# Half-width products in A's last stage, fourteen C blocks by crossbar loads, chunk 13 in quarters

## The chip, the cores and the metric

The kernel runs on one core of a Trainium2 chip. The metric is the device time of one execution in microseconds. Engines named here: PE (matrix products; "PEld" its weight loads), DVE (vector engine), ACT (scalar engine, which here mostly copies results from the matrix engine's banks to on-chip memory: an eviction), POOL and SP, of which both issue transfers. SP's queue issues loads and the last stores, POOL's the stores in between.

## The reference

Two heads over S = 2048 positions and D = 1024 channels stand side by side in the output, A in the left 1024 columns and B in the right ones.

```python
# A: a short causal filter, a product, a long convolution by FFT over 2S, a skip, a gate
for t in range(4):
    k_shift = k_shift + k_pad[:, t:t + S, :] * shift_k[:, 3 - t]
kv = k_shift * v
y = irfft(rfft(pad(kv)) * rfft(pad(ssm_k)))[:, :S, :]
a = q * (y + kv * ssm_D)
# B: a diagonal complex recurrence between two matrix products
Lam_bar = exp(dt * Lam);  B_bar = ((Lam_bar - 1) / Lam)[:, None] * Bmat
Bu = einsum("bld,pd->blp", x, B_bar)
h[t] = Lam_bar * h[t - 1] + Bu[:, t]
b = 2 * einsum("blp,dp->bld", h, Cmat).real + x * Dskip
out = concatenate([a, b], axis=-1)          # (1, 2048, 2048) bf16
```

## The kernel before

**Head B** goes through x in 16 chunks of 128 positions. `x` loads a chunk transposed (a crossbar load, L425). `U.i.jp.jl` multiplies it with B (16 products of 128x128x128, L444), `ue` evicts. On DVE, `r1`/`r2` rotate the result (L459, L466), `cy` on ACT carries the last column of the chunk before (L468), two `sc` are the scans (L472), `r3`/`r4` rotate back (L459, L478). `y.i.dh.part` multiplies with C and adds the diagonal skip (four products of 128x128x512 and one of 128x128, L527 and L530), `ye` evicts, `yst`, `ysp` or `yh` store. For chunks 6 to 12, `yt.i.s.part` does the same in quarters of the matrix engine: sixteen products of 64x64x512 (L498), after the last part of a half sixteen of 64x64x64 (L512). Between the halves s = 0 and s = 1 two row groups change banks; the kernel waits there for an eviction named by `yf`, or, where no `yf` stands, for a drain of PE (L488).

**B and C** come as 128x1024 blocks. Each of the sixteen B blocks is loaded (`bl`, L402), transposed by eight products with the identity (`bT`, L397) and evicted (`bc`, L413). C has sixteen blocks (d = 0..7, real and imaginary): eight go the same way (`cl` L417, `cT` L397, `cc` L421), eight by a crossbar load straight into place (`cx`, L419). All y and yt of an output half need the four d blocks of that half.

**Head A** has three stages with a trip through DRAM after each of the first two. Stage one: `kp`, `vp` load k and v; `kvm`, `kva`, `kvb`, `kvc` on DVE make kv for each of 16 slices n2 (L563 to L578); `am` is the first transform (L583), `ae` evicts, `ast` stores to `Ys_kv` (POOL, L592). The filter goes through `hl`, `hT`, `hc`, `hm`, `he`, `hst` to `Ys_h`. Stage two: `lh`, `lk` reload by frequency (SP, L639; each needs all sixteen stores), `sh`, `sk` transform (L650), `she`, `ske` evict (L660, L667), `sw` swaps rows by a transfer (POOL, L671), `pr` multiplies on DVE (L677), `sa` is the first half of the way back (L689), `sae` evicts, `vst` stores to `Vs` (L700). Stage three: `vl` reloads one n2 (SP, L705; each needs all sixteen stores), `a3` is the last transform with the constant `Gt` (two products of 128x128x512 per half, L717), `a3e` evicts (L724), `qp` loads q (L710), `qm` and `qh` gate on DVE (L726, L730), `osp` and `oh` store (SP, L734, L732).

`Gt[:, p, :]` holds nonzero columns only where the column's parity is p; the two products of an `a3` fill all 128 columns each and add up in one bank.

What sets the order is `ORDER`, a list of some 1,500 words written into the program. Each word is one task; the letters and numbers behind a colon give the slots that it takes: `a` a unit of a 53-unit arena in on-chip memory, `p` one of eight banks, `w` a weight slot, `h` a state slot. Each engine runs its tasks in the order of the list and waits only for data and slots, so the list is every engine's queue.

Of the kernel before, what the change touches and what calls it, by code (L numbers as in the profile page):

```python
# [16 lines left out]
BF16 = mybir.dt.bfloat16  # L17
# [15 lines left out]
def a_constants():  # L33
# [6 lines left out]
    G = np.stack([tr.T * (m % 2 == p)[None, :] * 2 / NFFT for p in range(2)], axis=1)  # L40
# [31 lines left out]
bc.3.0 bl.1.1:a44 bT.1.1:p3 sin1 kva.2 kvb.2:a34 bl.7.1:a46 bT.7.1:p4 bc.3.1 bl.4.0:a45 bT.4.0:p6 bl.7.0:a1 U.0.1.1 bc.1.1 U.0.0.1 bc.7.1 bT.7.0:p7
bc.4.1 bc.4.0 kvb.1:a1 sin2 x.5:a32 U.5.0.0:a50p3 U.5.0.1 U.5.1.0:p4 U.5.1.1 U.5.3.0:p6 bc.7.0 U.5.3.1 U.0.3.1 bl.5.1:a33 bT.5.1:p1 eo ue.5.1 vp.1:a48
bc.5.1 kp.-2 kvm.0:a44 kvc.2 ue.0.3 cl.0.1:a10 kvc.3 cl.1.1:a11 cT.1.1:p7 x.1:a0 U.1.0.0:a48p4 bl.5.0:a9 cx.5.1 kva.0 ue.5.0 bT.5.0:p1 bc.5.0 U.1.0.1
ue.1.0 cT.0.1:p2 cc.0.1 ue.5.3 U.1.2.0:p1 U.1.2.1 cc.1.1 U.1.3.0:p4 U.5.2.0:p6 U.0.2.0:p2 U.0.2.1 stt z2 U.5.2.1 z1 ue.0.1 x.2:a37 ue.0.0 kp.2
kvm.5:a28 kvm.4:a8 vp.0:a38 kvc.1 U.2.0.0:a42p3 U.2.2.0:p7 kvb.0:a36 U.2.3.0:p5 U.2.3.1 U.1.1.0:p0 cl.1.0:a40 kva.4 ue.0.2 r1.0:a4 ue.1.2 ue.5.2 kva.5
gz U.1.1.1 r2.0:h0 dd U.2.1.0:p2 ue.2.3 cx.4.0 am.1.0:p6p5 kvb.5:a41 cx.6.1 rt U.1.3.1 cl.0.0:a33 cT.0.0:p1 sc.0.1 U.2.1.1 ae.1.1.0:a2 ue.1.1 cc.0.0
cl.3.0:a16 cT.3.0:p5 ue.1.3 U.2.2.1 sc.0.0 r1.1:a28 ue.2.1 am.3.1:p4p1 cx.7.0 cc.3.0 ae.1.0.0 r3.0:a16 r2.1:h1 am.1.1:p2p0 ae.1.1.1 r4.0 U.2.0.1
ue.2.0 kvc.0 cT.1.0:p5 cl.2.0:a44 cT.2.0:p6 cc.1.0 x.3:a45 U.3.0.0:a46p0 U.3.2.0:p3 cc.2.0 cl.2.1:a5 cT.2.1:p5 U.3.0.1 cc.2.1 cl.3.1:a4 cT.3.1:p6
ae.3.0.1:a48 ue.2.2 U.3.2.1 ae.1.0.1 am.2.0:p4p5 cc.3.1 U.3.1.0:p2 cx.6.0 U.3.3.0:p7 y.0.0.0:p6 y.0.0.1 r1.2:a16 U.3.3.1 cx.7.1 cy.1 ae.2.0.0:a6  # L80
sc.1.1 sc.1.0 ae.2.1.0 am.2.1:p4p5 ue.3.3 ae.2.0.1 ue.3.0 y.0.0.2 y.0.0.3 kvb.4:a44 am.0.0:p4p7 r3.1:a28 ue.3.2 ae.0.0.0:a4 ae.0.1.0 U.3.1.1 cx.5.0
cx.4.1 y.0.1.0:p0 ue.3.1 vp.2:a38 y.0.1.1 y.0.1.2 kp.3 ae.2.1.1 y.0.1.3 am.3.0:p3p4 kvc.5 am.0.1:p7p2 r4.1 ae.0.0.1 ae.3.1.0 y.1.0.0:p5 ae.0.1.1
ae.3.1.1 kvc.4 y.1.1.0:p7 am.4.0:p4p2 y.1.0.1 y.1.1.1 r2.2:h2 y.1.1.2 hl.1:a42 y.1.1.3 r1.3:a8 ye.0.0:a40 y.1.0.2 cy.2 ae.3.0.0 sc.2.1 am.4.1:p1p3
ae.4.1.0:a38 y.1.0.3 ast.2 sc.2.0 hl.0:a34 r3.2:a28 hl.2:a6 r4.2 r2.3:h0 ye.0.1 ye.1.1:a33 am.5.0:p6p2 ae.4.0.0 ae.4.0.1 ae.4.1.1 ye.1.0 ae.5.0.0:a0
hl.3:a16 hT.0.6:p4 hT.0.5:p7 hc.0.5:a52 ae.5.1.0 hT.0.7:p0 hT.0.3:p5 hT.0.2:p1 hT.0.1:p3 hm.0.5.1:p6p7 x.13:a36 kp.4 y.2.1.0:p2 y.2.1.1 hc.0.2:a44
kvm.8:a28 he.0.5.1.1:a18 he.0.5.1.0 cy.3 hm.0.5.0:p1p7 lw.3:w1 sc.3.0 y.2.0.0:p6 kvm.9:a8 y.2.0.1 sc.3.1 kva.8 y.2.0.2 yst.0 y.2.1.2 he.0.5.0.1
hc.0.1:a52 he.0.5.0.0 kva.9 am.5.1:p7p3 ae.5.0.1 hT.0.4:p1 y.2.1.3 hc.0.4:a47 ast.3 ld_G hT.0.0:p7 ae.5.1.1 y.2.0.3 hc.0.6:a46 ye.2.1:a48 ast.1 xs.13
hm.0.2.0:p3p1 he.0.2.0.0:a2 x.4:a40 U.4.0.0:a6p4 U.4.0.1 ue.4.0 ye.2.0 U.4.1.0:p2 he.0.2.0.1 x.12:a49 hst.0.5.1 hc.0.7:a41 ast.4 U.4.1.1 hm.0.2.1:p3p4
U.4.3.0:p1 U.4.3.1 hst.0.5.0 U.4.2.0:p6 U.4.2.1 yst.1 r3.3:a36 kvb.8:a33 kvb.9:a44 r4.3 kvm.7:a8 ast.0 he.0.2.1.1 ue.4.1 xs.12 hc.0.3:a49
hm.0.3.1:p4p0 he.0.2.1.0 kvm.6:a28 y.3.0.0:p2 ue.4.3 he.0.3.1.0:a34 ue.4.2 he.0.3.1.1 hm.0.1.1:p3p5 he.0.1.1.1:a42 hm.0.3.0:p1p4 y.3.1.0:p6  # L90
hm.0.4.0:p0p5 y.3.1.1 kva.7 x.14:a16 he.0.3.0.1 hc.0.0:a49 kva.6 he.0.1.1.0 hm.0.1.0:p4p7 lw.2:w3 y.3.0.1 he.0.3.0.0 he.0.1.0.1 he.0.1.0.0
# [8 lines left out]
he.1.6.0.0:a46 hst.0.4.1 he.1.6.0.1 hm.1.6.1:p7p4 hT.1.3:p6 he.1.0.0.1:a44 hm.1.0.1:p0p5 he.1.0.0.0 kva.10 hst.0.4.0 hT.1.4:p3 y.4.0.2 he.1.6.1.0  # L100
hT.1.7:p7 hc.1.3:a41 he.1.0.1.0 y.4.1.3 he.1.6.1.1 hc.1.7:a33 hst.0.3.1 he.1.0.1.1 hst.0.0.0 hst.0.0.1 vp.5:a4 kvb.10:a0 kp.7 kvm.11:a8 kva.11 x.6:a35
kvb.11:a34 kvc.11 am.11.1:p0p4 am.11.0:p6p7 y.4.0.3 ae.11.1.1:a30 ae.11.0.1 hT.1.5:p5 ae.11.1.0 ae.11.0.0 kvc.10 am.10.0:p4p0 ae.10.0.0:a4 hst.0.6.0
ae.10.1.0 U.6.0.0:a2p7 am.10.1:p6p4 U.6.0.1 ye.4.0:a34 hm.1.1.0:p0p2 ye.4.1 he.1.1.0.1:a18 ast.6 U.6.2.0:p1 U.6.2.1 he.1.1.0.0 hst.1.6.0 hm.1.3.0:p0p2
# [4 lines left out]
hm.1.4.1:p2p5 he.1.4.1.0 vp.7:a44 vp.6:a30 he.1.3.1.0 y.5.0.1 y.5.0.2 y.5.0.3 ye.5.1:a52 hm.1.5.1:p4p6 he.1.4.1.1 he.1.7.0.0 hm.1.5.0:p7p1
he.1.5.0.1:a40 kvm.12:a36 he.1.5.0.0 kvc.15 kva.12 am.15.1:p3p5 x.7:a46 U.7.0.0:a8p2 he.1.5.1.0 U.7.0.1 ye.5.0 lw.0:w2 am.15.0:p1p7 kvc.13 U.7.1.0:p0
he.1.5.1.1 am.13.0:p4p6 ue.7.0 ast.10 kvb.12:a16 kvm.14:a36 ae.15.0.1:a32 hst.1.1.0 ae.15.1.0 am.13.1:p2p3 x.9:a11 ae.13.1.0:a4 kvc.12 U.9.0.0:a30p7  # L110
U.9.0.1 ae.13.0.1 U.7.2.0:p6 ae.13.1.1 U.7.2.1 x.15:a10 hst.1.2.0 am.12.0:p3p2 ae.13.0.0 ae.15.0.0 kva.14 U.7.1.1 r1.6:a12 kvb.14:a0 r2.6:h0 kvc.14
am.14.0:p4p1 cy.6 ae.12.1.0:a2 ae.12.0.0 sc.6.1 ue.9.0 U.7.3.0:p2 am.14.1:p7p3 hst.1.7.1 ue.7.2 U.9.2.0:p6 ae.15.1.1 ae.14.0.1:a44 U.7.3.1 hst.1.1.1
hst.1.2.1 ue.7.1 hst.1.3.1 am.12.1:p7p0 U.9.1.0:p5 U.9.1.1 ae.14.1.1 ae.14.0.0 ae.14.1.0 U.9.2.1 ue.7.3 ae.12.1.1 hst.1.4.1 hst.1.3.0 sc.6.0 yst.4
# [53 lines left out]
def full_kernel(ctx, tc, A_q, A_k, A_v, A_shift_k, A_ssm_k, A_ssm_D, B_x, B_Lre, B_Lim, B_Bre, B_Bim,  # L167
# [631 lines left out]
```

## Time and profile before

| | |
|---|---|
| three timed runs | 348.27, 350.30, 350.78 us; median 350.3 |
| the profiled execution | 351.36 us, of it 349.6 between the first and the last instruction; granted PE clock 0.995 |
| PE, DVE, ACT, POOL busy | 334.9, 314.1, 285.2, 79.4 us |
| transfers | 103.07 MB; hardware queue 63.98 MB, software queue 38.42 MB |

A row of groups names the line, engine, operation, output and inputs, how many, then busy us and the mean ns of one, and after the bar the idle time before them:

```profile
L472 DVE TENSOR_TENSOR_SCAN gslot<-rtab,gslot 128x1040 bf16<-128x1040 f32 x32 | 73.0, 2310 | 3.0 <-ACT gslot L468 2.8
L717 PE MATMUL bank<-arena,Gt 128*128 128x512 bf16 x62 | 14.5, 379 | 0.1
L421 ACT COPY CT<-bank 128x1024 bf16<-128x1024 bf16 x8 | 8.3, 1052 | 1.0 <-PE bank L397 1.0
```

A product's 379 ns runs from its start to its modelled end; since products overlap, the distance from one start to the next is what the engine pays, and that is read from the chain or the timeline. An instruction of SP or POOL that issues a transfer is shown with the time for which it held that queue; the landing comes later.

### The profile page before, as it was taken

To read this page: it belongs to the slowest core of one execution; us is meant where nothing else is said; L and a number is where in the kernel's file an instruction comes from. 1 tells how busy PE (TensorE), PEld (TensorE's weight loads), DVE (VectorE), ACT (ScalarE), POOL (GpSimd) and SP (SyncE) were. 2 spreads that over 40 slices of the span, in tenths; PEclk is the share of its full clock that TensorE was granted. 3 is DMA by queue.
4 is the path that set the end of the run, shared out by engine and by line. 5 is a ranking of instruction groups with operands and counts; after the bars stand their busy time and mean duration, and the time that the engine had idled before them with its cause. 6 is when DMAs were issued, how large, how long until landed. Compare 5 with 4: busy or idle time off the path is not lost. (4 is left out here: it accounts for less than half of the span.)

```text
span 349.6 us, 10684 instructions
## 1 busy us (share of the span) xinstructions
PE 334.9 (96%) x4540; PEld 236.7 (68%) x4561; DVE 314.1 (90%) x240; ACT 285.2 (82%) x547; POOL 79.4 (23%) x130
## 2 busy tenths in 40 slices
PE   5899999999999999999987999999999999999996
PEld 3799998546765767748863565786668676865442
DVE  4899999999999999999996997979985968997992
ACT  6999997468698999987884889999998887537672
POOL 5000000032334337055231004223233151300100
PEclk9999999999999999999998999999999999999999
DMA  6999967599999999999869599989989999779977
GB/s 204 336 297 257 239 157 79 225 263 281 289 317 295 370 273 316 314 259 303 301 229 367 181 335 310 364 304 347 384 322 321 368 400 344 281 264 389 344 299 266
DMA packets 63691, 103.07 MB, mean 295 GB/s; under 512 B 29550, under 2 KB 31870, under 8 KB 63644
## 3 DMA queue, kind: packets, MB, share of 16 engines
q1 hardware_dynamic: 52348, 63.98, 61.6%
q0 software_dynamic: 11296, 38.42, 30.0%
q8 instruction: 35, 0.57, 0.7%
q14 instruction: 12, 0.10, 0.1%
HBM read 53.09 MB, written 34.60 MB: 251 GB/s over the span
## 5 line engine op out<-in xcount | busy, mean ns | idle before, releaser
L444 PEld LDWEIGHTS <-BT 128*128 128x128 bf16 x2048 | 117.5, 98 | 11.3 <-issue 4.5
L444 PE MATMUL bank<-arena,BT 128*128 128x128 bf16 x2048 | 123.2, 219 | 1.2 <-ACT arena L446 0.5
L472 DVE TENSOR_TENSOR_SCAN gslot<-rtab,gslot 128x1040 bf16<-128x1040 f32 x32 | 73.0, 2310 | 3.0 <-ACT gslot L468 2.8
L527 PE MATMUL bank<-CT,gslot 128*128 128x512 bf16 x279 | 68.4, 379 | 0.7 <-DVE gslot L478 0.2
L498 PE MATMUL bank<-CT,gslot 64*64 64x512 bf16 x896 | 57.4, 384 | 0.0
L446 ACT CAST arena<-bank 128x512 bf16<-128x512 f32 x64 | 40.0, 659 | 13.3 <-PE bank L444 13.2
L677 DVE TENSOR_TENSOR arena<-arena 128x4096 bf16<-128x4096 bf16 x16 | 36.2, 2285 | 10.8 <-ACT arena L667 7.7
L527 PEld LDWEIGHTS <-gslot 128*128 128x128 bf16 x288 | 26.0, 98 | 27.8 <-DVE gslot L478 0.9
L667 ACT CAST arena<-bank 128x512 bf16<-128x512 f32 x64 | 38.5, 685 | 6.6 <-PE bank L650 6.6
L498 PEld LDWEIGHTS <-gslot 64*64 64x64 bf16 x896 | 29.8, 109 | 19.2 <-issue 1.7
L589 ACT CAST arena<-bank 128x512 bf16<-128x512 f32 x64 | 35.7, 632 | 7.8 <-PE bank L583 6.0
L459 DVE TENSOR_TENSOR arena<-arena,Z 128x4096 bf16<-128x4096 bf16 x16 | 36.5, 2282 | 4.7 <-ACT arena L446 4.2
L660 ACT CAST arena<-bank 128x512 bf16<-128x512 f32 x64 | 37.7, 731 | 3.5 <-PE bank L650 3.4
L627 ACT CAST arena<-bank 128x512 bf16<-128x512 f32 x64 | 36.2, 632 | 4.8 <-PE bank L621 4.7
L697 ACT CAST arena<-bank 128x512 bf16<-128x512 f32 x64 | 38.7, 738 | 0.9 <-PE bank L689 0.9
L459 DVE TENSOR_TENSOR arena<-gslot,Z 128x4096 bf16<-128x4096 bf16 x16 | 36.6, 2289 | 1.0
L671 POOL DMA_DIRECT2D arena<-arena x32 | 17.4, 546 | 79.5 <-ACT arena L660 75.3
L563 DVE TENSOR_TENSOR arena<-arena 128x4096 bf16<-128x4096 bf16 (+3 forms) x16 | 30.0, 1885 | 1.2 <-DMA arena<-in_A_k_dram 0.7
L592 POOL DMA_DIRECT2D Ys_kv<-arena x16 | 11.4, 719 | 86.2 <-ACT arena L589 86.2
L630 POOL DMA_DIRECT2D Ys_h<-arena x32 | 23.2, 737 | 24.9 <-ACT arena L627 24.9
L650 PE MATMUL bank<-arena,wslot 64*64 64x512 bf16 x256 | 24.3, 388 | 3.6 <-DMA arena<-Ys_kv 3.2
L536 ACT CAST arena<-bank 128x512 bf16<-128x512 f32 x32 | 20.1, 651 | 8.4 <-PE bank L530 4.7
(101 smaller groups left out, 414.6 us busy)
## 6 DMA issues: line engine op xcount, KB each, us to landing
Ys_kv<-arena POOLq DMA_DIRECT2D x16, 512.0 KB, 5.6
Ys_h<-arena POOLq DMA_DIRECT2D x32, 256.0 KB, 4.7
arena<-Ys_h SPq DMA_DIRECT2D x16, 512.0 KB, 5.5
arena<-arena POOLq DMA_DIRECT2D x32, 256.0 KB, 4.8
arena<-Ys_kv SPq DMA_DIRECT2D x16, 512.0 KB, 6.3
Vs<-arena POOLq DMA_DIRECT2D x16, 512.0 KB, 5.5
arena<-Vs SPq DMA_DIRECT2D x16, 512.0 KB, 7.1
arena<-in_A_k_dram SPq DMA_DIRECT2D x8, 512.0 KB, 6.0
```

The lines of the kernel that those rows point to most:

```text
L444: nc.tensor.matmul(pu[:, w, jl, :], BT[:, 2 * jp + jl, w, d, :], xT[:, d, :], start=(d == 0), stop=(d == ND - 1))
L446: E["ue"] = lambda i, jp: nc.scalar.copy(st["u", i][:, :, 2 * jp:2 * jp + 2, :], st.pop(("pu", i, jp)))
L459: nc.vector.tensor_mul(m, s_, win(Z))
L472: nc.vector.tensor_tensor_scan(gf, rtab[:].rearrange("p j t -> p (j t)"), gf, 0.0, ALU.mult, ALU.add)
L498: mm = nc.tensor.matmul(st["py", i, dh][64 * c:64 * c + 64, :], h[rows, w, j, 2 + 64 * c:66 + 64 * c], CT[rows, j, w, dh * 512:(dh + 1) * ...
L527: nc.tensor.matmul(py, h[:, w, j, 2:GW], CT[:, j, w, dh * 512:(dh + 1) * 512], start=(j == 0 and w == 0), stop=False)
L589: return nc.scalar.copy(st["ysb", n2][:, p, dh * 512:(dh + 1) * 512], st.pop(("pa", n2, p, dh)))
L627: return nc.scalar.copy(st["yh", hf, s][:, p, e, :], st.pop(("pb", hf, s, e, p)))
L660: return nc.scalar.copy(st["hab", i][:, 0, a, l, :], st.pop(("ps", "h", g, l)))
L667: return nc.scalar.copy(st["x16", i][:, a, l, :], st.pop(("ps", "k", g, l)))
L677: nc.vector.tensor_mul(hab, st.pop(("x16", i)).rearrange("p a l d -> p (a l d)").unsqueeze(1).to_broadcast([P, 2, 2 * D]), hab)
L697: return nc.scalar.copy(st["vsb", i][:, a, dh * 512:(dh + 1) * 512], st.pop(("pv", g, dh)))
```

## The change

1. `a3`: `Gt[:, p, :]` keeps only its 64 nonzero columns. Each of the two products of an `a3` is 128x64x512 and writes its own 64 partitions of the bank, with no adding up. Row m = 2k + p of the result now lies in partition 64p + k.
2. Therefore q is loaded, and A's output stored, in two transfers of 64 partitions with every second row of DRAM each, where one transfer stood before (`qp`, `oh`, `ost`, `osp`).
3. Six more C blocks (d = 1, 2, 3, both parts) come by crossbar load: `cl`, `cT` and `cc` of these are gone, six `cx` are new. Two blocks (d = 0) keep the old way.
4. Chunk 13's products with C are `yt` in place of `y`, without a `yf`, so with PE's drain in the middle.
5. The raw parameters are loaded into a weight slot instead of a tile of their own.
6. `ORDER` is a new list: order and slots of nearly all tasks differ.

```diff
-    G = np.stack([tr.T * (m % 2 == p)[None, :] * 2 / NFFT for p in range(2)], axis=1)
+    G = np.stack([tr.T[:, m % 2 == p] * 2 / NFFT for p in range(2)], axis=1)
...
-        praw = const.tile([4 * NJ, P], BF16, name="praw")
+        praw = wslots[1][0:4 * NJ, 0:P]
...
         st["qt", r] = sb(2).rearrange("p (s d) -> p s d", s=2)
-        spd(st["qt", r], qr[:, 2 * r:2 * r + 2, :])
+        for p in range(2):
+            spd(st["qt", r][64 * p:64 * p + 64, :, :], qr[p::2, 2 * r:2 * r + 2, :])
...
         for p in range(2):
-            nc.tensor.matmul(pt, Gt[:, p, :], st["vv", n2][:, p, dh * 512:(dh + 1) * 512], start=(p == 0), stop=(p == 1))
+            nc.tensor.matmul(pt[64 * p:64 * p + 64, :], Gt[:, p, :], st["vv", n2][:, p, dh * 512:(dh + 1) * 512], start=True, stop=True)
...
+    def halves(dma, rows, tile):
+        for p in range(2):
+            dma(rows[p::2], tile[64 * p:64 * p + 64])
-    E["osp"] = lambda r: spd(oar[:, 2 * r:2 * r + 2, :], st["ot", r])
+    E["osp"] = lambda r: halves(spd, oar[:, 2 * r:2 * r + 2, :], st["ot", r])
```

The words of the two lists that the prediction speaks of. Start of SP's queue, up to r1.0, before:

```
ld_par bl.6.0 bl.1.0 bl.0.0 bl.0.1 bl.2.1 bl.2.0 kp.1 bl.6.1 kp.0 bl.3.1 bl.3.0 x.0 kp.-1 bl.4.1 bl.1.1 bl.7.1 bl.4.0
bl.7.0 x.5 bl.5.1 vp.1 kp.-2 cl.0.1 cl.1.1 x.1 bl.5.0 cx.5.1 x.2 kp.2 vp.0 cl.1.0
```

and after:

```
bl.3.0 ld_par bl.4.0 bl.0.0 bl.2.1 bl.4.1 bl.2.0 bl.0.1 bl.3.1 kp.-2 kp.0 kp.-1 cx.6.0 bl.1.1 bl.1.0 x.0 kp.1 bl.6.1
cx.1.0 bl.7.0 x.5 kp.2 x.1 cx.2.0 bl.7.1 cx.7.1 bl.6.0 vp.1 bl.5.1 bl.5.0 cx.5.0 cl.0.0 vp.0 cl.0.1 cx.1.1 x.2 cx.3.1
cx.5.1 x.3 cx.7.0 cx.2.1 vp.2 cx.3.0 cx.6.1 cx.4.0
```

The hand-over from A's stage one to stage two, before: the last kv words are `kvc.14 am.14.0 ... am.14.1 ... am.12.1 ... ae.12.1.1 ... ae.12.0.1`, POOL's last stores `ast.13 ast.15 ast.14 ast.12`. After:

```
kvb.12 hst.1.4.0 ae.14.1.1 kvc.12 am.12.1 ae.14.0.1 ae.14.1.0 am.12.0 hst.1.2.1 hst.1.4.1 ue.7.0 ae.14.0.0 hst.1.3.0 ue.7.3
x.9 U.9.0.0 U.9.0.1 U.9.3.0 ae.12.0.1 ae.12.0.0 ae.12.1.1 ... ae.12.1.0 ... ast.15 ... ast.13 ... ast.14 lh.3 ... lw.0 ast.12
... lh.0 ... x.15 ... lh.1 ... lk.1 sk.2
```

The tail on DVE, from r1.13 to r4.15, before: r1.13 r2.13 sc.13 sc.13 r3.13 r4.13 r1.14 ... r4.14 qh.14 qm.2 r1.15 r2.15 sc.15 sc.15 r3.15 qm.1 r4.15. After:

```
r1.13 r2.13 sc.13.1 sc.13.0 r3.13 r4.13 r1.14 r2.14 sc.14.1 sc.14.0 r3.14 r4.14 qm.2 r1.15 r2.15 qm.3 sc.15.1 sc.15.0 qh.14
r3.15 qm.5 r4.15
```

Behind it come all eight parts of y.15, in both lists. Behind the last word of stage two on PE (sa.25) the new list has U.15, U.14, yt.12, yt.13, then four runs of a3 with U.15 and y.14 between, then y.15.

More of the change, by code (lines that the diff above doesn't have):

```diff
@@ L72 @@
[L72 to L79, printed above, removed]
@@ L100 @@
[L100 to L103, printed above, removed]
@@ L108 @@
[L108 to L111, printed above, removed]
```

181 lines of the change are left out of this document (98 added, 83 removed).

## The prediction

> **What bounds the kernel now.** I read the busy time of each engine by windows first, since this program passes through stages with different limits.
>
> ```profile
> 90.00:110.00 20.00, 19.89 (x198) 13.51 (x200) 20.00 (x18) 17.86 (x32) 5.96 (x9) 1.00 1.07 309
> ...
> 180.00:185.00 5.00, 2.90 (x68) 2.29 (x64) 4.91 (x3) 2.71 (x6) 2.34 (x5) 1.00 0.89 265
> 185.00:190.00 5.00, 5.00 (x68) 2.41 (x64) 3.22 (x3) 3.02 (x7) 0.00 (x0) 0.66 1.03 377
> ...
> 210.00:230.00 20.00, 19.41 (x349) 13.18 (x344) 16.81 (x8) 20.00 (x43) 5.17 (x9) 1.00 0.97 334
> ```
>
> The columns are PE, weight loads, DVE, ACT, POOL, granted clock, DMA share. From 30 to 170 us DVE never stops (20.00 of 20), from 210 to 250 us ACT never does, and between them, at 180 to 195, everything waits. PE is high throughout but sets the pace only where nothing else does: at the end. The timeline of the hand-over shows the wait:
>
> ```profile
> 164.37 0.68 DVE L578 TENSOR_TENSOR arena<-arena 128x1024 bf16<-128x1024 bf16 x1
> ...
> 171.51 1.16 ACT L589 CAST arena<-bank 128x512 bf16<-128x512 f32 x2
> ...
> 172.96 0.69 POOL L592 DMA_DIRECT2D Ys_kv<-arena  x1 [0.78 <-ACT arena L589]
> ...
> 179.51 1.43 SPq L639 DMA_DIRECT2D arena<-Ys_kv  x3
> ...
> 184.73 0.63 PE L650 MATMUL bank<-arena,wslot 64*64 64x512 bf16 x8 [2.10 <-DMA arena<-Ys_kv]
> ```
>
> The last kv product (kvc.14) ends at 165.05, yet the last eviction of A's first stage (ae.12.0.1) ends at 172.67: am.12.1 stands late in PE's order. Only then go its store, the reload and `sk`; every `lk` needs all sixteen stores. The chain that ended last, and DVE's timeline, show the end:
>
> ```profile
> 334.59 4.32 PE bank L717 x20
> 338.91 0.86 PE bank L527 x4
> ...
> 346.30 0.58 ACT arena L536
> ```
>
> ```profile
> 296.00 2.29 DVE L459 TENSOR_TENSOR arena<-arena,Z 128x4096 bf16<-128x4096 bf16 x1 [0.22 <-issue]
> ...
> 335.40 1.22 DVE L478 TENSOR_TENSOR gslot<-arena 128x2048 bf16<-128x2048 bf16 x1
> ```
>
> The 296.00 row is r1.13, the 335.40 row r4.15. Chunk 15 could have been multiplied with C from 336.62, but twenty A products held PE until 338.91. From r1.13 to the end are 349.6 - 296.0 = 53.6 us.
>
> **The change, part by part.** The sum is made against the profiled execution (span 349.6, run 351.36), which lies 1.06 above the median 350.3; I subtract the gain from the median.
>
> *Half-width products.* The 64 products of L717 come every 0.216 us (20 in 4.32): 13.8 us. After, 64 products fill half the columns each, two at a time. Nearest rows: quarter products with different moving data in the two column groups (L650, L689) run four at once, 16 in 0.99 us. So a pair costs between 0.216 (together) and 0.432 us (one after the other); I take 0.216, PE loses 6.9 us. Three of their four runs stand between full-width work. In the trace the step from a full to a quarter product takes 0.149 instead of 0.056 us; seven such borders cost 0.7 us, or nothing.
>
> *Six C blocks by crossbar.* Gone are 48 transposes (L397, 0.06 each back to back: 2.9 us of PE) and six evictions of L421 (1.04 each, 0.95 back to back: 5.7 us of ACT). All lie at 30 to 57 us beside a DVE that does not pause: worth nothing by themselves. They cost SP's queue:
>
> ```profile
> 24.97 4.37 SPq L419 DMA_TRANSPOSE CT<-in_B_C_im_dram  x1
> ...
> 41.45 0.33 SPq L417 DMA_DIRECT2D arena<-in_B_C_re_dram  x1
> ```
>
> The eight holds of L419 average 2.15 us, the eight of L417 0.52. Six swaps are 9.8 us of queue, in a stretch where the DMA share is 1.08 to 1.20. Ahead of the last B load (bl.5.0, issued at 24.3) there now stand four crossbar loads (cx.6.0, 1.0, 2.0, 7.1) and one k pair more, two C loads less: 4 x 2.15 + 0.48 - 2 x 0.52 = 8.0 us later. The v pairs behind it go likewise: vp.1 issues about 30.9 instead of 17.9 and lands near 36.5 at its 5.3 us. DVE's cover: the order gives it all six kvm, kva and kvb ahead of the first kvc, until about 34.5. So it waits about 2 us there; against that, the 1.1 us that DVE idled at 12.85 and 26.84 (0.70 and 0.38) find work in this order. I take +1.0 for r1.0, counted beyond the 2.6 us of kv work (kva, kvb, kvc: 1.21 + 0.68 + 0.68) that it now has before it. Bounds: 0 (hidden) and the whole 9.8 (no cover).
> [...]
>
> *The order made anew: hand-over.* kvc.12 is now the last kv product, at the same 150.8 us of DVE work as kvc.14 was, so at 165.05. am.12.1 and am.12.0 follow at once in PE's order, their evictions in ACT's behind five that are ready before: 165.05 + 0.4 + 0.4 + 4 x 0.51, and a short wait, gives about 168.2, 4.5 us before 172.67. POOL issues ast.13, 14 and 12 (0.69 each) behind eleven smaller stores, ready by then; these stores and x.7, x.10, x.9 now share 150 to 170 us (share was 0.7 to 0.98), so ast.12 may land 1 us later than its issue promises. On SP, `lk` stands behind lh.0 and x.15 (1.24 to 3.8 us of hold, while ast.12 is in flight). I take -3.5; bounds -4.5 and 0.
>
> *Between hand-over and r1.13.* From the first `sk` to pr.13 the work in the two orders, added up at the rows' durations, differs little: PE 102.9 to 101.3, ACT 114.2 to 115.9 (evictions at 0.55), DVE 102.8 in both. The stretch took 111 us, and ACT idled for some 9 of it. I take 0, bounds -3 and +4, since every slot is dealt anew.
>
> *The tail.* Behind pr.13, PE has 43.8 us of work (before it was 50.8 from 296.0 on). DVE from r1.13 to r4.15: three times (2.29 + 1.22 + 4.54 + 2.29 + 1.22) = 34.7, three qm of 1.22, qh.14 0.69, about 1 of gaps: 40.0. Then y.15 (8 x 0.92), ye 0.6, yh 0.3 + 2.3: 50.6 in all. PE alone would need 43.8 + 3.3 = 47.1, so DVE now sets the end, and the transfers come close: the sixteen V loads (512 KB) go back to back at share 1.0 from 306 to 330, so 1.5 us each. The first `vl` issued 10 us after r1.13, behind the last vst, and does so again (last eviction about 4.5 us after r1.13, before 5.6). Sixteen loads, seven A stores of 1.5, six pieces of 0.75: 24 + 10.5 + 4.5, 10 ahead and 2.3 to land = 51.3 if never idle. I take 51.5: -2.1; bounds 0 and -3.0. So of the 6.9 us saved on PE two thirds are idle time.
>
> *Small things.* Chunk 13 in quarters: sixteen take 0.86 us, the diagonal 0.12 twice, 7.1 against 7.4 us; its PE drain in the middle costs at most one product's 0.38. Both off the path. q loads: eight more issues at L710's 0.37 us, put where SP waits anyway; A's stores nine more at 0.49: osp is paced by qm (1.22 against 0.98 for two), and at the very end oh.15's second half stands before yh.15.0: 0 to 0.5, taken as nothing. praw's new home and the halved G: nothing; the parameter loads stand behind one B load, 0.4 us, under the 3.6 that DVE waits there.
>
> Sum: +1.0 - 3.5 + 0 - 2.1 = -4.6: 350.3 - 4.6 = **345.7 us** (the profiled span 345.0).
>
> **Rivals.**
> *The tail does not shorten* (halves one after the other, 6.9 us back on PE: 50.7 + 3.3 = 54.0; or V loads and stores hold it at 53.6): 350.3 + 1.0 - 3.5 + 0.4 = 348.2. For it: the DMA share of 1.0. Against: L650's pace.
> *The hand-over comes no sooner*, because ast.12 queues behind the stores ahead of it: 350.3 + 1.0 - 2.1 = 349.2. For it: share 0.98 at 150 to 160. Against: the before paid this too.
> *Slower: the start starves.* The crossbar loads hold SP's queue, DVE stands before kvc.3 and kvc.0 for the full 9.8 us, and all of DVE's unbroken stretch moves: 350.3 + 9.8 - 3.5 - 2.1 = 354.5. It decides where vp.0 lands after about 51 us instead of my 42. For it: one hold of 4.37 us, share 1.2. Against: most holds are under 2 us, and C blocks 3.0, 6.1 and 4.0 follow r1.0's loads.
> *The crossbar loads cost nothing*: the holds only reflect a queue that the transfers fill anyway, and vp.1 lands in time: term 0, 344.7. [...] Against: 2.15 against 0.52 us in the same stretch. [...]
>
> **How the numbers follow.** Chances: forecast 0.56, free crossbar 0.08, tail 0.12, hand-over 0.10, starved start 0.14. One per cent is 3.5 us, about what a measurement tells here: faster means below 346.8, slower above 353.8. The forecast's own bounds (339.8 with every term at its good end, 350 with stage two 4 us worse) put 0.42 below and 0.14 within; free crossbar 0.07 and 0.01; tail 0.03 and 0.09; hand-over 0.02, 0.07 and 0.01 slower; starved start 0.14 slower. Together 0.54, 0.31, 0.15. The range reaches from 339.5 to 354: half of the starved start and a little below are left out; the forecast alone would be 341 to 350.
>
> **What would show it.** Right: r1.0 at about 46 us (42.5); DVE at 20.00 of 20 from 46 to 170; the first `sk` near 182 (184.7); r1.13 near 293.5 (296.0); L717's successor about 7 us busy in all; y.15 starting directly behind r4.15, with PE idle before it. Wrong: r1.0 after 50 (start starved), lk's issue still at 179 (no hand-over gain), the first `vl` more than 12 us after r1.13, or a wait of DVE between 60 and 160 us, which the order made anew could bring and nothing above prices.

## The result, and the profile after

Nine timed runs of the changed kernel have a median of 354.31 us (352.85 to 357.0), nine of the kernel before 350.3 (347.79 to 356.82). The ratio is 1.0134 with a 95% interval of 1.0093 to 1.0176: slower by about 4.7 us, where 4.6 us less were forecast. The ratio compares mean times and leaves out the one execution of the kernel before, at 356.82 us, that fell into a slower state. The tables below give ratios to the kernel before on the same chip; one per cent is 3.5 us. The profiled execution took 353.56 us, 351.8 of it between the first and the last instruction (before: 351.36 and 349.6). Line numbers shift by one or two from kernel to kernel.

The first lines come from the list of groups (busy us, mean ns of one, and after the bar the idle time before them); the last of them is the kernel before:

```profile
L717 PE MATMUL bank<-arena,Gt 128*64 128x512 bf16 x64 | 8.6, 384 | 2.7 <-DMA arena<-Vs 2.7
L676 DVE TENSOR_TENSOR arena<-arena 128x4096 bf16<-128x4096 bf16 x16 | 36.2, 2284 | 11.5 <-DMA arena<-arena 9.5 <-ACT arena L666 1.8
L677 DVE TENSOR_TENSOR arena<-arena 128x4096 bf16<-128x4096 bf16 x16 | 36.2, 2285 | 10.8 <-ACT arena L667 7.7 <-PE bank L498 1.9 <-ACT arena L660 1.2
```

The half-width products do run in pairs: L717 takes 8.6 us in all where it took 14.5. But L717 now waits 2.7 us for the V reload, where 0.1 us of idle time stood before it. DVE's product L676 idles hardly more than before, 11.5 against 10.8 us; what ended the wait is another thing, mostly the swaps by transfer (9.5 us) in place of evictions.

The hand-over, from the timeline (start, us):

```profile
168.50 2.05 ACT L588 CAST arena<-bank 128x512 bf16<-128x512 f32 x4
...
170.85 0.69 POOL L591 DMA_DIRECT2D Ys_kv<-arena  x1 [1.99 <-ACT arena L588]
...
171.42 0.39 SPq L638 DMA_DIRECT2D arena<-Ys_h  x1
...
175.85 1.25 SPq L638 DMA_DIRECT2D arena<-Ys_kv  x2
...
179.76 0.41 PE L649 MATMUL bank<-arena,wslot 64*64 64x512 bf16 x4
...
192.15 4.49 DVE L676 TENSOR_TENSOR arena<-arena 128x4096 bf16<-128x4096 bf16 x2 [1.46 <-DMA arena<-arena]
```

and DVE's product in the kernel before:

```profile
191.12 4.49 DVE L677 TENSOR_TENSOR arena<-arena 128x4096 bf16<-128x4096 bf16 x2 [2.87 <-ACT arena L667]
```

A's stage one ends sooner than before, but by less than forecast: its last eviction at 170.6 (172.67 before, 168.2 forecast, or 169.2 with the 1.0 us that the start was to lose). The first kv reload `lk` is issued at 175.85, 3.7 us sooner than 179.51. Yet pr.0, the first product of DVE behind it, starts at 192.15 where it started at 191.12. The gain is gone within 16 us.

The end, first from the chain that ended last (start, us, what):

```profile
319.30 11.55 DMA arena<-Vs
330.90 0.84 PE bank L717 x6
...
336.04 1.58 ACT arena L724 x3
337.66 1.02 PE bank L526 x4
...
345.21 0.59 ACT arena L535
```

The same stretch in the timeline of SP's queue (start, time held):

```profile
336.62 8.68 SPq L735 DMA_DIRECT2D out_dram<-arena  x10
345.40 0.98 SPq L538 DMA_DIRECT2D out_dram<-arena  x1
346.47 1.32 SPq L735 DMA_DIRECT2D out_dram<-arena  x2
347.88 0.54 SPq L538 DMA_DIRECT2D out_dram<-arena  x1
```

A V load issued at 319.30 takes 11.55 us to land, no longer than others do (up to 11.1 us in the kernel before, 11.9 in `a_qsone` below), but the a3 products behind it have to wait for it. They run late, then y.14 and sixteen more of them, and y.15 starts at 337.66, 2.3 us behind r4.15 (335.32). The last eviction ends at 345.80, a whole 1.1 us sooner than before (346.88). But the span ends 6.0 us behind it, where that took 2.7: ten halves of A's stores take up SP's queue for 8.68 us, the last store of B is issued 2.1 us after its data is there, and the transfers themselves take longer.

That they do is seen in windows (the last three columns are granted clock, DMA share, GB/s). The kernel before:

```profile
338.00:346.00 8.00, 7.95 (x43) 3.81 (x42) 4.99 (x5) 3.16 (x7) 0.00 (x0) 1.00 0.90 335
```

The changed kernel, for the same 8 us and for the 14 us of most q loads:

```profile
282.00:296.00 14.00, 13.88 (x253) 11.23 (x244) 11.83 (x6) 12.58 (x26) 3.71 (x6) 1.00 0.99 311
338.00:346.00 8.00, 7.17 (x40) 3.33 (x37) 4.19 (x4) 4.31 (x9) 0.00 (x0) 1.00 0.89 266
```

At the end the engines for transfers are as busy as before (0.89 and 0.90) and move a fifth less, 266 in place of 335 GB/s. A busy share alone says nothing of that: the bytes must be read beside it.

### The profile page after: what moved, and what is told of

Same layout as the page of the kernel before. It is cut to its first block, busy times and chain, and to the rows that moved or that the text cites. A ratio compares the mean times of both kernels' runs of the same rounds, so it can differ in the third digit from the quotient of the medians.

```text
span 351.8 us, 10830 instructions
## 1 busy us (share of the span) xinstructions
PE 329.0 (94%) x4633; PEld 232.0 (66%) x4633; DVE 314.3 (89%) x240; ACT 279.3 (79%) x541; POOL 79.8 (23%) x130
## 4 chain that ended last, share of the span: by engine, by line
PE 57%; DVE 14%; ACT 12%; DMA 11%; issue 2%; SPq 1%; POOL 0%; DVEq 0%; ACTq 0%
PE bank L443 19%; PE bank L526 15%; PE bank L497 8%; ACT arena L696 4%; DMA arena<-arena 4%; PE bank L620 4%; PE bank L582 3%; DVE arena L562 3%; DMA arena<-Vs 3%; ACT arena L659 3%; ACT arena L666 2%; DMA arena<-in_A_k_dram 2%; PE bank L604 2%; PE bank L688 2%; DVE arena L458 2%
## 5 line engine op out<-in xcount | busy, mean ns | idle before, releaser
L497 PE MATMUL bank<-CT,gslot 64*64 64x512 bf16 x1024 | 63.2, 377 | 0.3
L526 PE MATMUL bank<-CT,gslot 128*128 128x512 bf16 x256 | 61.5, 379 | 0.1
L445 ACT CAST arena<-bank 128x512 bf16<-128x512 f32 x64 | 40.2, 644 | 15.8 <-PE bank L443 15.7
L497 PEld LDWEIGHTS <-gslot 64*64 64x64 bf16 x1024 | 32.6, 107 | 22.2 <-issue 1.1
L676 DVE TENSOR_TENSOR arena<-arena 128x4096 bf16<-128x4096 bf16 x16 | 36.2, 2284 | 11.5 <-DMA arena<-arena 9.5
L626 ACT CAST arena<-bank 128x512 bf16<-128x512 f32 x64 | 35.5, 641 | 5.8 <-PE bank L620 5.0
L696 ACT CAST arena<-bank 128x512 bf16<-128x512 f32 x64 | 36.1, 656 | 4.5 <-PE bank L688 4.4
L588 ACT CAST arena<-bank 128x512 bf16<-128x512 f32 x64 | 35.8, 654 | 4.5 <-PE bank L582 4.3
L526 PEld LDWEIGHTS <-gslot 128*128 128x128 bf16 x256 | 23.1, 98 | 24.6 <-issue 0.6
L666 ACT CAST arena<-bank 128x512 bf16<-128x512 f32 x64 | 37.5, 690 | 1.9 <-PE bank L649 1.3
L659 ACT CAST arena<-bank 128x512 bf16<-128x512 f32 x64 | 35.7, 697 | 0.7 <-PE bank L649 0.6
L535 ACT CAST arena<-bank 128x512 bf16<-128x512 f32 x32 | 19.1, 623 | 17.2 <-PE bank L511 9.1
L629 POOL DMA_DIRECT2D Ys_h<-arena x32 | 24.1, 775 | 35.3 <-ACT arena L626 29.9
L649 PE MATMUL bank<-arena,wslot 64*64 64x512 bf16 x256 | 23.0, 384 | 0.8 <-ACT arena L659 0.3
```

What stands on the lines that cost most here:

```text
L445: E["ue"] = lambda i, jp: nc.scalar.copy(st["u", i][:, :, 2 * jp:2 * jp + 2, :], st.pop(("pu", i, jp)))
L497: mm = nc.tensor.matmul(st["py", i, dh][64 * c:64 * c + 64, :], h[rows, w, j, 2 + 64 * c:66 + 64 * c], CT[rows, j, w, dh * 512:(dh + 1) * ...
L526: nc.tensor.matmul(py, h[:, w, j, 2:GW], CT[:, j, w, dh * 512:(dh + 1) * 512], start=(j == 0 and w == 0), stop=False)
L588: return nc.scalar.copy(st["ysb", n2][:, p, dh * 512:(dh + 1) * 512], st.pop(("pa", n2, p, dh)))
L659: return nc.scalar.copy(st["hab", i][:, 0, a, l, :], st.pop(("ps", "h", g, l)))
L666: return nc.scalar.copy(st["x16", i][:, a, l, :], st.pop(("ps", "k", g, l)))
```

## The experiments

Two theories stood at the start. One: the transfers of 64 partitions, which part 2 brought, cost more than part 1 saves. The rival: the parts are good, and the new order of the 1,500 words loses.

### The parts, each alone

`b_half` is the kernel before with parts 1 and 2, `b_cx` the kernel before with part 3, `b_all` the kernel before with parts 1 to 4, all in the old order; `a_full` is the changed kernel with parts 1 and 2 undone. The edits are the change's own lines, and for `b_cx` words like these:

```diff
-cl.1.1:a11 cT.1.1:p7 cc.1.1
+cx.1.1
```

> The kernel before with parts 1 and 2 alone (half-width products, q loads and A's stores in two halves of 64 partitions), its own order kept. Theory (the halves take back at the last stores what they save on PE): the twenty A products ahead of y.15 take about 2.5 us in place of 4.32, so y.15 starts about 1.8 us sooner, but the last stores, of which a third of the 2-KB packets took 120 to 300 ns against 84 in the trace of the changed kernel, end about 5 us behind the last eviction in place of 2.7: in all 0 to +1 us. Rival (the parts are good and only the new order loses): the stores add nothing and the time falls by about 2 us, to some 348.

> The kernel before with part 3 alone: six C blocks by crossbar loads at the places where their plain loads stood. Theory: a small price at the start, r1.0 about 1 us later and the whole +0.5 to +1.5 us. Rival one (the crossbar loads starve the start): +4 us or more, with r1.0 after 47 us. Rival two (they cost nothing): within 0.5 us.

> Parts 1 to 4 in the order and the slots of the kernel before (chunk 13's sixteen quarter products where its products stood, six crossbar loads where the plain loads stood). Theory (the parts themselves bring nothing, and the new order is not the main loss): the sum of the two runs with one part each, 0 to +2.5 us. Rival (the new order is the whole loss): about 3 us faster than before, some 347.

> The changed kernel with parts 1 and 2 undone (full-width products, one transfer for each q load and A store), in the new order. Theory (halves give back at the stores what PE gains): PE has about 6 us more work in the tail of which 2.8 us fill its idle time, so y.15 starts about 3 us later than 337.7, and the last stores end about 3 us sooner behind the last eviction: within 1 us of the changed kernel, 354. Rival (the half-width products gain what the sum took, 2.1 us or more, and other steps lose it): 2 to 4 us slower than the changed kernel, 356 to 358. Second rival (the halves are a loss in themselves): 2 us or more faster than the changed kernel.

| run | order | parts | ratio | interval |
|---|---|---|---|---|
| changed kernel | new | all | 1.0134 | 1.0093 to 1.0176 |
| b_half | old | 1, 2 | 1.0134 | 1.0080 to 1.0187 |
| b_cx | old | 3 | 0.9990 | 0.9959 to 1.0021 |
| b_all | old | 1, 2, 3, 4 | 1.0167 | 1.0094 to 1.0239 |
| a_full | new | 3, 4 | 1.0052 | 1.0026 to 1.0078 |

Parts 1 and 2 alone, in the old order, lose as much as the whole change, more than the theory gave. The rival falls: the old order with all parts is no better. Undoing the two parts in the new order takes back 0.8 per cent, so `a_full`'s second rival fits best: the halves are a loss in themselves. (`b_all`'s ratio rests on three executions only.) The six crossbar loads cost nothing that could be measured, against the theory's +0.5 to +1.5 us. In the old order SP's queue at the end shows the same as in the new one:

```profile
336.72 11.00 SPq L736 DMA_DIRECT2D out_dram<-arena  x12
347.82 0.54 SPq L539 DMA_DIRECT2D out_dram<-arena  x1
348.46 1.94 SPq L736 DMA_DIRECT2D out_dram<-arena  x2
350.48 0.54 SPq L539 DMA_DIRECT2D out_dram<-arena  x1
```

The twelve halves take up SP's queue for 11.00 us, and the end comes 7.9 us behind the last eviction (346.03 to 353.95).

### A mend that failed: split by slice

The halves could be avoided if each transfer took one slice over all 128 partitions. The rows of DRAM then come in the order p, k (`slices` is the function that holds the `dma` line; q's loads are split alike):

```diff
-        for p in range(2):
-            dma(rows[p::2], tile[64 * p:64 * p + 64])
...
+        dma(oar[:, n2, :].rearrange("(k p) d -> p k d", p=2), tile)
...
+        for s in range(2):
+            slices(dma, 2 * r + s, st["ot", r][:, s, :])
```

> The changed kernel with its half-width products kept, but q's loads and A's stores split by slice in place of by half: two transfers of 256 KB as in the change, each over all 128 partitions (the DRAM rows taken in the order 'p k'). Theory (it is the transfers over 64 partitions that lose, not their number nor the products): the last store ends about 3 us behind the last eviction in place of 6.0, the 2-KB packets of the stores all take about 84 ns, the q loads no longer hold stage two, so r1.13 comes near 294 in place of 296.1; y.15 starts within 1 us of r4.15; in all 5 us under the changed kernel, 348 to 349. Rival one (more transfers are what costs): as the changed kernel, 354. Rival two (the half-width products bring nothing): as with parts 1 and 2 undone, 351.6.

> The changed kernel with q's loads alone split by slice over 128 partitions; A's stores stay halves of 64 partitions. Theory: the q packets (238 ns on the mean at 281 to 297 us against 159 for most before) fall back, stage two's swaps land sooner, r1.13 about 2 us sooner than 296.1, while the last stores still end about 6 us behind the last eviction: 351 to 352.5. Rival (q's loads lie where nobody waits, as predicted): no change, 354.

> The changed kernel with A's stores alone split by slice over 128 partitions; q's loads stay halves. Theory: r1.13 stays at 296, and the end comes about 3 us sooner: 350.5 to 351.5. Rival (the last stores wait for SP's queue by their number, eight more holds): no change at the end, 354.

> The order and slots of the kernel before, with half-width products, transfers split by slice over 128 partitions, and the six more crossbar loads. Theory (parts 1 and 3 are good once no transfer covers 64 partitions only): y.15 starts directly behind r4.15, about 2 us sooner than before, nothing else moves: about 347.5, 0.5 to 1 per cent under the kernel before. Rival (the end of the tail is set by the V loads and the stores, not by PE): as the kernel before, within 0.3 per cent.

The ratios were 1.4015 (both), 1.2072 (q loads alone), 1.2007 (stores alone) and 1.3945 (both, old order). No theory had that. The run with only the stores so split shows why, first in a window:

```profile
360.00:380.00 20.00, 0.00 (x0) 0.00 (x0) 0.00 (x0) 0.00 (x0) 0.00 (x0) 0.50 0.13 51
```

and in its SP queue:

```profile
350.06 46.56 SPq L734 DMA_DIRECT2D out_dram<-arena  x10
```

All compute has ended, and the share is 0.13, two sixteenths, at 51 GB/s; ten stores of 256 KB hold the queue 46.56 us, and each 2-KB packet takes the usual 84 ns. The profile takes its share over sixteen engines, so this is as much as two of them would give. What these transfers have and A's other q loads and stores lack is a DRAM side whose outermost size is 2. That this size is the cause was not shown: no run varies it alone.

### What the halves cost, without that trap

If the rows may leave in another order, whole transfers of 128 partitions need no split at all. The runs of this kind give up the reference's row order: A's rows are gated with q's rows in another order, or leave in another order, and the rest is computed as before. `a_qone` has the q loads of the kernel before, `a_sone` its stores, `a_qsone` both, each in the changed kernel. `a_2q` issues the second half of each store from POOL, and `a_halfrow` keeps halves of 64 partitions, but with 64 neighbouring rows.

```diff
 # a_2q
-        for p in range(2):
-            dma(rows[p::2], tile[64 * p:64 * p + 64])
+        for p, d in enumerate((dma, gpd)):
+            d(rows[p::2], tile[64 * p:64 * p + 64])
 # a_halfrow
-            dma(rows[p::2], tile[64 * p:64 * p + 64])
+            dma(rows[64 * p:64 * p + 64], tile[64 * p:64 * p + 64])
...
-            spd(st["qt", r][64 * p:64 * p + 64, :, :], qr[p::2, 2 * r:2 * r + 2, :])
+            spd(st["qt", r][64 * p:64 * p + 64, :, :], qr[64 * p:64 * p + 64, 2 * r:2 * r + 2, :])
```

> The changed kernel with each q load as one transfer over 128 partitions in DRAM's row order; A is then gated with q's rows in another order, all else is computed as before. A's stores stay halves. Theory (q's loads over 64 partitions hold stage two's transfers): the q packets fall from 238 ns towards 160 on the mean, r1.13 comes about 2 us sooner than 296.1, the last stores still end about 6 us behind the last eviction: 351 to 352.5. Rival (q's loads lie where nobody waits, as predicted): no change, 354.

> The changed kernel with each A store as one transfer over 128 partitions in the tile's own order; A's rows then leave in another order, all else is computed as before. q's loads stay halves. Theory (stores from 64 partitions hold the end): all 2-KB store packets take about 84 ns, the last store ends about 3 us behind the last eviction in place of 6.0: 350.5 to 351.5. Rival (the end is set by PE and the V loads): no change, 354.

> The two together: half-width products, whole q loads and whole A stores; A's rows are gated and leave in another order. Theory: what part 1 is worth without the price of part 2: both gains add up, y.15 starts within 1 us of r4.15, 348 to 349, and about 3 us under the changed kernel with parts 1 and 2 undone (351.6). Rival (half-width products bring nothing even so): 351 to 352.

> The changed kernel with the second half of each A store issued from POOL's queue in place of SP's, so that both halves of a tile leave at the same time from all 128 partitions. Theory (packets are slow because 16 engines read the same 64 partitions; and SP's queue holds the last store by 2.1 us): the last store ends about 4 us behind the last eviction, 352. Rival (a transfer over 64 partitions is slow in itself, whatever runs beside it): no change in the packets' times and at most 1 us gained by the shorter queue.

> The changed kernel with the halves kept at 64 partitions each, but with neighbouring DRAM rows (the first 64, the last 64) in place of every second row; A's rows are gated and leave in another order. Theory (64 partitions are what makes the packets slow): as the changed kernel, 353 to 355, q packets near 238 ns. Rival (the wider step between DRAM rows makes them slow): packets near 160 ns, and the time near 347 to 348.

The packet times in the table are counted from the traces: the mean ns of the 4-KB packets of the hardware queue at 270 to 296 us, which are q loads, and of its 2-KB packets from 338 us on, which are stores, with the part of them that took 120 ns or more. `a_2q` sends half of its stores over the other queue, so its packets are not set beside these.

| run | ratio | interval | q packets | store packets |
|---|---|---|---|---|
| before | 1 | | 185 | 88, 2% |
| changed kernel | 1.0134 | 1.0093 to 1.0176 | 237 | 109, 29% |
| a_qone | 1.0019 | 0.9996 to 1.0043 | 195 | 109, 28% |
| a_sone | 1.0030 | 0.9996 to 1.0063 | 235 | 87, 1% |
| a_qsone | 0.9928 | 0.9896 to 0.9959 | 188 | 87, 1% |
| a_halfrow | 1.0147 | 1.0109 to 1.0185 | 240 | 109, 30% |
| a_2q | 1.0119 | 1.0063 to 1.0175 | | |

This settles the main cause. Whole q loads take back 1.15 per cent (4.0 us), whole stores 1.04 (3.6 us), both 2.06 (7.2 us), each to within some 1.8 us, and with both the change is faster than the kernel before, by 0.7 per cent. `a_sone` came out as its theory had it and `a_halfrow` nearly so; `a_qsone` is 1 us better than its theory. It is the 64 partitions and not the distance of the rows in DRAM: with neighbouring rows packets and time stay as bad (240 ns for the q packets and a ratio of 1.0147 in `a_halfrow`). Nor is it the size of a transfer: `a_qsone`'s last A store (L731 below, issued at 340.15) moves 256 KB over 128 partitions, as much as one of the halves, and its 128 packets take 85 ns on the mean, none of them 120. That there are twice as many transfers may add to the price; no run separates it. Why the packets of these transfers are slower (237 ns in the changed kernel's q loads, 188 in `a_qsone`'s) no run shows. Sending the two halves of a tile from two queues, as `a_2q` does, gained nothing measurable: its ratio lies in the changed kernel's interval and above the 352 us (1.0045) of its theory.

The window of the q loads in `a_qone`:

```profile
282.00:296.00 14.00, 13.88 (x235) 11.09 (x230) 11.66 (x7) 12.58 (x26) 3.92 (x6) 1.00 0.96 344
```

and that of the last stores in `a_sone`:

```profile
338.00:346.00 8.00, 5.66 (x32) 2.61 (x30) 3.53 (x4) 2.93 (x6) 0.00 (x0) 1.00 0.82 301
```

With whole q loads the same stretch moves 344 in place of 311 GB/s at a lower share; with whole stores 301 at 0.82 in place of 266 at 0.89. One expectation for `a_qone` was wrong: r1.13 hardly moved (295.8 against 296.1). A part of the q loads' price is paid further on. The last `vst`, issued at 300.2 and 300.3, lands at 304.6 and not 306.6, so the V reload starts sooner, and y.15 starts right behind r4.15 (335.38 and 335.22).

The stretch from r1.13 to the end shows the price best, since it repeats well: 53.6, 53.6 and 53.8 us in the kernel before, `b_cx` and `b_cxyt` (a run further below). With halves it takes 57.9 in `b_half` and 55.7 in the changed kernel; with whole q loads 53.9, with whole stores 51.6, with both 50.3. So all that whole stores gain lies there, and 1.8 of the 4.0 us of the q loads; where the rest of these lies is open.

The end of `a_qsone` in the timeline of SP's queue, with y.15's first products on PE below:

```profile
332.29 6.35 SPq L733 DMA_DIRECT2D out_dram<-arena  x5
339.71 0.34 SPq L538 DMA_DIRECT2D out_dram<-arena  x1
340.15 0.41 SPq L731 DMA_DIRECT2D out_dram<-arena  x1
341.50 0.33 SPq L538 DMA_DIRECT2D out_dram<-arena  x1
...
333.34 1.02 PE L526 MATMUL bank<-CT,gslot 128*128 128x512 bf16 x4
```

Its r4.15 ends at 333.18 and y.15 starts 0.16 us later; each last store is issued as soon as its data is there, and the span ends 2.7 us behind the last eviction.

### The order, and the hand-over

`b_qsonecx` is `a_qsone`'s products and transfers with part 3 in the old order. `a_qsoneU` and `a_fullU` move three words behind stage two's first products:

```diff
-U.9.1.0:p1 ast.13 U.9.1.1 ast.14 lh.3:a48 sh.6:p6p7 ... ue.9.1 ... sh.7:p4p5 she.7.0 she.7.1
+ast.13 ast.14 lh.3:a48 sh.6:p6p7 ... sh.7:p4p5 U.9.1.0:p1 U.9.1.1 she.7.0 she.7.1 ue.9.1
```

> The order and slots of the kernel before with half-width products, the six more crossbar loads, and whole q loads and A stores; A's rows are gated and leave in another order. Theory (the new order itself is a loss of about 1.5 us, as 351.6 against 349.2 hints): 345.5 to 346.5, under the 347.2 of the same parts in the new order. Rival (the new order brings the hand-over's gain, which the old list lacks): 348 to 349.5.

> The changed kernel with whole q loads and A stores (rows in another order) and two words moved on PE: the 32 products of U.9.1 stand behind sh.6 and sh.7 in place of ahead of them, its eviction behind theirs. Theory (the hand-over's gain was eaten because 192 U products stood ahead of stage two's first product on PE and its evictions then came in one unbroken row): sh.6 starts about 1.8 us sooner than 179.8, the first swap and pr.0 (192.15) 1 to 1.5 us sooner, and the time falls by 0.5 to 1.5 us against 347.2. Rival (ACT and the transfers pace stage two, whatever pr.0 does): pr.0 sooner, the time the same within 0.3 us. Second rival (lk's landing still sets it): pr.0 no sooner.

> The changed kernel with parts 1 and 2 undone and U.9.1 moved behind sh.6 and sh.7; nothing left out. Theory: 0.5 to 1.5 us under the 351.6 of the same kernel without the move, 350 to 351. Rival: no change, 351.6.

| run | order | ratio | interval |
|---|---|---|---|
| a_qsone | new | 0.9928 | 0.9896 to 0.9959 |
| b_qsonecx | old | 0.9973 | 0.9942 to 1.0004 |
| a_qsoneU | new, U.9.1 moved | 0.9959 | 0.9931 to 0.9987 |
| a_full | new | 1.0052 | 1.0026 to 1.0078 |
| a_fullU | new, U.9.1 moved | 1.0091 | 1.0056 to 1.0127 |

The theory that the new order is a loss as such does not hold. With full-width products it is slower than the old one (`a_full` 1.0052 against `b_cx` 0.9990, intervals apart); with half-width products and whole transfers it is rather faster (0.9928 against 0.9973, though the intervals overlap a little). The time of `b_qsonecx` is what its rival gave, but not for the rival's reason: the difference shows in the tail, 52.7 us from r1.13 to the end against 50.3, and not in the hand-over. In `a_full` sixteen full products of A stand ahead of y.15, as PE's timeline shows:

```profile
334.18 3.62 PE L716 MATMUL bank<-arena,Gt 128*128 128x512 bf16 x16
337.64 0.59 PE L526 MATMUL bank<-CT,gslot 128*128 128x512 bf16 x2
```

r4.15 ended at 333.7, so y.15 lost 3.9 us there.

Moving the U products gained nothing, in two kernels. The theory was that 192 of them (168.95 to 179.83) kept stage two's first product from starting. In `a_qsoneU` PE was free earlier, and then waited (its timeline):

```profile
179.54 0.41 PE L649 MATMUL bank<-arena,wslot 64*64 64x512 bf16 x4 [1.43 <-DMA arena<-Ys_h]
```

pr.0 came no sooner, at 192.79. What sh.6 waits for is the filter's reload `lh`. Before, the last filter store landed at 166.4, `lh` was issued at 166.6, and the first such product ran at 173.6; in the changed kernel that store lands at 171.4, and `lh` goes out at 171.42. So in these two profiles the new order brings the kv reload 3.7 us sooner and the filter's reload 4.8 us later, and now both fall together. The window 175 to 180 us of the kernel before:

```profile
175.00:180.00 5.00, 5.00 (x93) 3.22 (x94) 4.57 (x4) 4.32 (x10) 1.49 (x3) 1.00 0.50 199
```

and of the changed kernel:

```profile
175.00:180.00 5.00, 5.00 (x91) 4.80 (x92) 4.97 (x4) 1.95 (x5) 0.00 (x0) 1.00 1.30 255
```

Where the engines for transfers were half idle (0.50), they are now full (1.30), and the first `lk` takes 8.4 us to land (175.8 to 184.2) where it took 5.2 (179.5 to 184.7). It arrives half a microsecond sooner than before.

One profile of each kernel is little to go by here, but up to pr.0 other runs share these lists. In the seven profiles with the old list, `lh` is first issued at 165.5 to 170.3, `lk` at 177.1 to 182.3, and pr.0 starts at 187.7 to 192.6, with a median of 188.9. In nine with the new list, U.9.1 not moved, the figures are 170.0 to 174.4, 175.8 to 179.7, and 191.4 to 194.0, with a median of 192.2. So the 3.7 us of `lk` are in part a lucky draw (the medians, 179.2 and 178.0, differ by 1.2), the late `lh` belongs to the order, and pr.0 comes some 3 us later in it, not sooner. That the one brings the other is argued, not shown.

The last two runs: `a_qsoneHU` is `a_qsoneU` with the last filter stores put in another order on POOL, `b_cxyt` is `b_cx` with part 4.

```diff
-hst.1.7.0 ... hst.1.5.1 hst.1.5.0 hst.1.2.0 hst.1.1.1 ast.15 hst.1.3.1 hst.1.7.1
+hst.1.2.0 hst.1.1.1 hst.1.3.1 hst.1.7.1 hst.1.5.0 hst.1.5.1 hst.1.7.0 ... ast.15
```

> The run with whole q loads, whole A stores (rows in another order) and U.9.1 moved, in which sh.6 waited 1.43 us for the filter's reload; and now POOL's last filter stores are put ahead of ast.15 and of hst.1.7.0, whose eviction is the last. Theory (the filter's reload came 5 us later in the new order than before, 171.4 against 166.6, and then fell together with the kv reload): the last filter store lands about 3 us sooner, lh issues near 169, sh.6 starts near 177.5 to 178 in place of 179.5, the first lk lands within 6 us of its issue in place of 6.3 to 8.4, pr.0 comes 1.5 to 2.5 us sooner than 192.8, and the time is 346 to 347.5, 1 to 2 us under the 348.5 of that run. Rival (stage two is paced by ACT and the transfers behind, not by its start): pr.0 sooner, the time within 0.4 us of 348.5.

> The kernel before with part 3 and part 4 (six more crossbar loads, chunk 13 in quarters), order and slots its own; nothing left out. Theory: part 4 changes nothing that can be measured, 349 to 349.8, as with part 3 alone (ratio 0.999). Rival: the drain of PE in the middle of chunk 13 delays r1.13's successors and the tail: 1 us or more slower.

`a_qsoneHU` came to 0.9937 (0.9904 to 0.9971), not to be told from `a_qsoneU`. It did not do what it was to do, as POOL's timeline shows:

```profile
166.45 3.61 POOL L629 DMA_DIRECT2D Ys_h<-arena  x5 [5.07 <-DMA Ys_h<-arena]
```

POOL stood 5.07 us before these stores, waiting for an earlier one to land, and `lh` was issued at 174.47, later still. Whether an earlier filter reload would have carried the gain through is therefore open. The changed kernel has a saturated stretch at 150 to 160 us (share 1.14 and 1.18; before 1.04 and 0.91), which may delay these stores; no run shows it. `b_cxyt` came to 0.9976 (0.9947 to 1.0005): part 4 changes nothing that can be measured. Of the kernels that keep A's row order, none came out clearly faster than the kernel before.

## Why the prediction was wrong

**The step that failed** is in "Small things": "q loads: eight more issues at L710's 0.37 us, put where SP waits anyway; A's stores nine more at 0.49 [...] 0 to 0.5, taken as nothing". It priced the split transfers by the time that their issue holds SP's queue. It did not ask what a transfer of 64 partitions costs the engines that carry it, and the trace of before held no such load or store of A's to tell. The runs show 4.0 us for the q loads and 3.6 for the stores, 7.2 together, of the 9.3 us between the forecast of 4.6 less and the 4.7 more that came. No rival had this mechanism; the tail rival, in which V loads and stores hold the end, left the stretch behind r1.13 at the 53.6 us of before, and it took 55.7. Even the holds were dearer than priced: the eighteen halves of A's stores hold SP for 0.70 us each on the mean, where 0.49 was taken. The other 2.1 us were forecast ahead of r1.13 and did not come, as the start and the hand-over below show.

**Half-width products.** Right. The two products of a pair start 3 or 4 ns apart in 28 of the 32 pairs (28 to 30 ns in the others), and inside a run one pair follows the other after 0.21 us, as taken. The first step of a run (0.24) and a pause of 0.4 before the last pair come on top: the run of sixteen takes 2.13 us, and with the 0.38 of the last one's length left out that is 0.25 us a pair. At that rate 64 products cost 8.0 us in place of 13.8, a saving of 5.8 and not 6.9.

**The tail.** Right where its transfers are whole: `a_qsone` takes 50.3 us from r1.13 to the end, a little better than the 51.5 forecast, and y.15 starts right behind r4.15. In the changed kernel DVE's part is as forecast as well (r1.13 to the end of r4.15 39.3 us, forecast 40.0). From r1.13 to the end it took 55.7 us, 4.2 over the forecast: y.15 began 2.3 late, and the end came 6.0 behind the last eviction where the sum had 2.6, together 5.7, against 0.7 saved on DVE and the 0.9 by which the forecast was taken above its own sum.

**The start.** r1.0 came at 46.26, forecast 46, but that is partly luck. The wait was elsewhere than thought: DVE stood 2.97 us before the first kvm for k, and not before kvc for v. And the last kv product ended at 167.82, 2.8 us later than before, where +1.0 was taken; what took the rest is open. (DVE's 20.00 of 20 "from 30 to 170 us" is the row at 90 to 110; from 110 to 170 it was already 19.8 before, and 90 to 110 gives 19.90 in the changed kernel.) The crossbar loads by themselves are cheaper than the term made them: `b_cx` is at 0.9990, at most 0.7 us above the kernel before. There they stand in the places of the plain loads, though, and not ahead of the last B loads as in the new order, which no run tests alone. The term came from the queue's holds; the landing times in the trace of before, 5.0 and 5.4 us by crossbar (medians of the imaginary and the real parts) against 5.6 and 5.2 plain, come nearer to what `b_cx` shows: in time the loads were as cheap there as plain ones, though the holds stay longer (the fourteen in the changed kernel average 1.71 us against 0.52 for a plain load before).

**The hand-over.** This term failed as well. With the start's +1.0 the forecast had `lk` issued 2.5 us sooner; 3.7 were measured, but by two errors that cancel and a lucky draw. The last kv product ended 1.8 us and the last eviction 1.4 us later than forecast, while the last store landed 4.9 us after its issue, where it took 6.4 before and 1 us more was allowed; the other profiles with the new list have `lk` up to 3.9 us later than this one. That the first `sk` would follow `lk` by the same time was wrong: 184.4, forecast 182, before 184.7. The step took the filter's reload as done by then, as it was before; its stores were named among the "eleven smaller stores, ready by then", but not that `lh` waits for the last of them.

**Between hand-over and r1.13.** Forecast 293.5; 296.1 in the changed kernel, 293.8 in `a_full` and 293.9 in `a_qsone`. This looks like a hit for the two with whole q loads, but `a_qone` has 295.8, and `b_cx`, whose time is the kernel before's, has 292.8 against 296.0. One profile of each does not carry a difference of 2 us at this place, and the times say only that the change without halves is 2.5 us faster (1.4 to 3.6) where 4.6 were forecast. Their tails alone, 50.3 against 53.6 us behind r1.13, differ by 3.3. So all that lies ahead of r1.13, forecast at 2.5 us less, brought no gain that can be seen; how that divides over start, hand-over and stage two stays open.

## What to carry to other kernels

When a layout is changed to save an engine work, price the transfers that must follow it by what they do to the bytes moved at a given busy share, and not by the time of their issue: here 5.8 us of products were bought with 7.2 us of transfers over 64 partitions. Look for every partition range and every outermost size that the edit gives to a transfer. And where a new order brings one reload forward, see which other reload stood in that time before.

## What the runs showed of the hardware

- A's q loads and stores over 64 partitions were slower than those over 128, with neighbouring rows of DRAM as with every second one: 4-KB load packets 235 to 240 ns on the mean against 185 to 195, and 28 to 30% of the 2-KB store packets at 120 ns or more against 1 to 2% (the runs of the table of packets).
- A's stores with a DRAM side that begins with a size of 2 ran at a share of 0.13 and 51 GB/s where they ran alone (`a_ssl`, 360 to 380 us), and sixteen of them made the ratio 1.20.
- Two products of 128x64x512 that write the two halves of a bank's partitions started 3 or 4 ns apart in 28 of 32 pairs, and such pairs followed one another every 0.21 us inside a run, as single products of full width did before (0.216). With the pauses of a run of sixteen it was 0.25 us a pair.
